# One kind of two-bank PSUM tile for an attention and gMLP stack, with the 64-row matmuls of the gMLP gathered into fewer runs

## The chip, the cores and the metric

The kernel runs on one core of one Trainium2 chip, in one launch. The metric is the device time in microseconds (us); the median of three runs of the kernel before is 1190.72 us (1190.54 to 1191.43). The engines are named as the profile names them: PE is TensorE (its matmuls), PEld its weight loads, DVE is VectorE, ACT is ScalarE, POOL is GpSimd, and SP issues DMAs.

## What is computed

Four layers on an activation x of 2048 rows by 576 columns, in the order A, B, A, B, with the same weights both times:

```python
x = x + _A_ref(_layernorm(x), A_wqkv, A_wo)
x = x + _B_ref(_layernorm(x), B_w_in, B_w_sp, B_b_sp, B_w_out)
x = x + _A_ref(_layernorm(x), A_wqkv, A_wo)
x = x + _B_ref(_layernorm(x), B_w_in, B_w_sp, B_b_sp, B_w_out)
```

Layer A is attention with 32 heads of 18 columns, in which each row looks at 8 earlier rows at a distance of 2. Layer B is a gMLP with Fh = 2304:

```python
z  = _gelu(x @ w_in)                 # 2048 x 4608
z1 = z[..., :Fh]
z2 = _layernorm(z[..., Fh:])
g  = einsum('ts,bsf->btf', w_sp, z2) + b_sp
return (z1 * g) @ w_out
```

## The kernel before

**Layer A** (`layer_A`) projects q and k (`PG`, tile `pp`) and v (`VW`, tile `pv`), and then walks through 38 half-steps, two for each of 19 row tiles. A half-step multiplies q and k into logits (`L_mm`, tiles `L_ps`), takes their exponential on ACT (`EXP`), multiplies by v (`PV`, tile `O_ps`), and fits in what is left of the projections and the output projection (`WO`, tile `pw`). The order of the instructions on each engine in layer A is the order in which the code is written (`tc.manual_schedule`).

**Layer B** (`layer_B`) has three stages. The first computes z2 for each of 16 tiles of 128 rows (`p1_main`, line 791), takes the gelu and sums on ACT (line 805), sums of squares on DVE (line 807) and ACT (line 809), and normalizes (`p1_norm`, DVE and POOL, lines 832 and 834). The second takes 9 blocks of 256 columns: z1 of a block with 128 columns at a time (`z1(jj, sub)`, line 869, gelu in line 881), and the spatial product for 512 rows at a time (`gate`, 16 matmuls in line 887, then two DVE instructions in lines 891 and 892). The third multiplies by w_out (`p3_mm`, line 941, tile `po`) and adds x (`p3_finish`, line 951). In layer B the framework's scheduler sets the order of the instructions.

**Semaphore waits** are drawn by the framework, which keeps account of which instruction reads and writes which tile. When a pool's slot is taken by a new tile, the first write to it waits until the last reader of the tile that was there before is through.

**PSUM** has 8 banks of 512 fp32 columns per partition. Here they are shared out once for the whole kernel: two slots of two banks (`H_tile`, tag "H", for `L_ps`, `pz`, `pz1`, `po2`), and four slots of one bank (`PT_tile`, tag "PT", for all else: `pp`, `pv`, `O_ps`, `pw`, the transposes `pt`, `pzs`, `pg`, `po`). Each `PT_tile` is a tile of its own. In layer A, 151 such one-bank tiles are written in the first layer and 146 in the second; most are read by a single DVE or ACT instruction, `O_ps` by two.

**The 64-row remainder.** The inner dimension of 576 is four times 128 and 64 more. The four full pieces are matmuls of 128 rows. [...] In the z2 stage a tile of 128 rows has five units (512, 512, 512, 512 and 256 columns): units 0 and 1 first with their full pieces, then the run of five remainders, then the full pieces of the other three. In z1 there are four units of 512 columns and a run of four remainders for each 128 columns.

Of the kernel before, what the change touches and what calls it, by code (L numbers as in the profile page):

```python
# [9 lines left out]
ACT = mybir.ActivationFunctionType  # L10
# [8 lines left out]
P = 128  # L19
D = 576  # L20
H = 32
# [41 lines left out]
class K:  # L63
# [135 lines left out]
    def H_tile(self, name):  # L199
        return self.ps.tile([P, 2, 512], f32, name=name, tag="H", bufs=2)  # L200

    def PT_tile(self, shape, dt, name):
        return self.ps.tile(shape, dt, name=name, tag="PT", bufs=4)
# [118 lines left out]
    def layer_A(self, li):  # L322
# [26 lines left out]
        if li == 0:  # L349
            w2 = R["win2a"][:].rearrange("p c n -> p (c n)")  # L350
            lent = [w2[:, k_ * 2 * CBW:(k_ + 1) * 2 * CBW].rearrange("p (a b) -> p a b", a=2) for k_ in range(2)]
        man = tc.manual_schedule(engines={ET.PE, ET.Activation, ET.DVE, ET.Pool, ET.SP})
# [370 lines left out]
    def layer_B(self, li):  # L723
# [7 lines left out]

        zu_cm = pool("zu")
# [19 lines left out]
        cchunks = []  # L752
        c0 = 0
        while c0 < Fh:
            cn = min(1024, Fh - c0)
            cchunks.append((c0, cn))
            c0 += cn
        ncch = len(cchunks)
        SQ_D = (Fh * 2 // 3) // 256 * 256
        units = []  # L760
        for ci, (c0, cn) in enumerate(cchunks):
            for sub in range((cn + 511) // 512):
                units.append((ci, c0, sub, min(512, cn - sub * 512)))
# [14 lines left out]
        def p1_main(i):  # L778
            zp = p1.tile([P, Fh], bf16, name="zp", bufs=3)
            sums = p1.tile([P, ncch + 2], f32, name="z_sums", bufs=3)  # L780
            pzvs = []
            for ci, (c0, cn) in enumerate(cchunks):
                if cn > 512:
                    pzvs.append(self.H_tile("pz")[:].rearrange("p a b -> p (a b)"))
                else:
                    pzvs.append(self.PT_tile([P, 512], f32, "pzs")[:, :])

            def z_mm(u, c, start, stop):
                ci, c0, sub, w = units[u]
                r0, r1 = (0, P) if c < 4 else (64 * (u % 2), 64 * (u % 2) + 64)  # L790
                nc.tensor.matmul(pzvs[ci][:, sub * 512:sub * 512 + w],  # L791
                                 lhsT=self.xnT[r0:r1, c, PADL + i * P:PADL + (i + 1) * P],
                                 rhs=win2(c)[r0:r1, c0 + sub * 512:c0 + sub * 512 + w],
                                 start=start, stop=stop, tile_position=(r0, 0))
            nu = len(units)
            for u in range(2):
                for c in range(4):
                    z_mm(u, c, c == 0, False)
            for u in range(nu):
                z_mm(u, 4, u >= 2, u < 2)  # L800
            for u in range(2, nu):
                for c in range(4):
                    z_mm(u, c, False, c == 3)
            for ci, (c0, cn) in enumerate(cchunks):
                nc.scalar.activation(out=zp[:, c0:c0 + cn], in_=pzvs[ci][:, 0:cn],  # L805
                                     func=ACT.Gelu_apprx_tanh, accum_out=sums[:, ci:ci + 1])
            nc.vector.tensor_tensor_reduce(out=spare[:, 0:SQ_D], in0=zp[:, 0:SQ_D], in1=zp[:, 0:SQ_D], scale=1.0,  # L807
                                           scalar=0.0, op0=ALU.mult, op1=ALU.add, accum_out=sums[:, ncch:ncch + 1])
            nc.scalar.activation(out=spare[:, SQ_D:Fh], in_=zp[:, SQ_D:Fh], func=ACT.Square,
                                 accum_out=sums[:, ncch + 1:ncch + 2])  # L810
            mean = p1.tile([P, 1], f32, name="z_mean", bufs=3)
            nc.vector.tensor_reduce(out=mean[:], in_=sums[:, 0:ncch], axis=AX.X, op=ALU.add)
# [5 lines left out]
            nc.vector.tensor_tensor(out=sq[:], in0=sums[:, ncch:ncch + 1], in1=sums[:, ncch + 1:ncch + 2], op=ALU.add)  # L818
# [18 lines left out]
        for i in range(NS):  # L837
            self.run_deferred(upto_row=(i + 1) * P)
            p1_main(i)
            if i == 0:  # L840
                self.run_deferred()
            if i == min(2, NS - 1):
                for q in range(NQ):
                    load_W(q)
                load_w1(0)
            if i == min(6, NS - 1):
                self.dma(bsp, self.B_b_sp.partition_broadcast(P), eng=nc.gpsimd)
            if i >= 1:
                p1_norm(i - 1)
# [11 lines left out]
        def z1(jj, sub):  # L861
            w1 = w1s[jj]
            z1T = p2.tile([P, S], bf16, name="z1T")
            z1Ts[jj, sub] = z1T
            pz1s = [self.H_tile("pz1") for _ in range(NQ // 2)]

            def mm(q, c, start, stop):
                r0, r1 = (0, P) if c < 4 else (64 * (q % 2), 64 * (q % 2) + 64)
                nc.tensor.matmul(pz1s[q // 2][:, q % 2, :], lhsT=w1[r0:r1, c, sub * P:(sub + 1) * P],  # L869
                                 rhs=self.xnT[r0:r1, c, PADL + q * 512:PADL + (q + 1) * 512],  # L870
                                 start=start, stop=stop, tile_position=(r0, 0))
            for q in range(2):
                for c in range(4):
                    mm(q, c, c == 0, False)
            for q in range(NQ):
                mm(q, 4, q >= 2, q < 2)
            for q in range(2, NQ):
                for c in range(4):
                    mm(q, c, False, c == 3)
            for q2 in range(0, NQ, 2):  # L880
                nc.scalar.activation(out=z1T[:, q2 * 512:(q2 + 2) * 512],  # L881
                                     in_=pz1s[q2 // 2][:, :, :].rearrange("p a b -> p (a b)"), func=ACT.Gelu_apprx_tanh)

        def gate(jj, sub, q):
            pg = self.PT_tile([P, 512], f32, "pg")
            for i in range(NS):
                nc.tensor.matmul(pg[:, :], lhsT=Z[:, jj, i, sub * P:(sub + 1) * P], rhs=Wq[q][:, i, :],  # L887
                                 start=(i == 0), stop=(i == NS - 1))
            qs = slice(q * 512, (q + 1) * 512)
            tmp = p2.tile([P, 512], f32, name="g_tmp", bufs=3)  # L890
            nc.vector.tensor_tensor(out=tmp[:], in0=pg[:, :], in1=bsp[:, qs], op=ALU.add)  # L891
            nc.vector.tensor_tensor(out=uT(jj)[:, sub, qs], in0=tmp[:], in1=z1Ts[jj, sub][:, qs], op=ALU.mult)  # L892

        for jj in range(NB):
            if jj + 1 < NB:
                load_w1(jj + 1)
            if 0 < jj < NB - 1:
                for sub in range(2):
                    z1(jj, sub)
                    for q in range(NQ):  # L900
                        gate(jj, sub, q)
            elif jj == 0:
                z1(jj, 0)
                z1(jj, 1)
                for sub in range(2):
                    for q in range(NQ):
                        gate(jj, sub, q)
            else:
                z1(jj, 0)
                z1(jj, 1)  # L910
                for q in range(NQ):
                    for sub in range(2):
                        gate(jj, sub, q)
# [48 lines left out]
        if NS >= 2 and JL > 0:  # L962
            accs = []
            for i in range(2):
                ht = self.H_tile("po2")
# [87 lines left out]
```

## The time and the profile before

| what | value |
|---|---|
| median of three runs | 1190.72 us |
| span of the profiled execution | 1190.8 us |
| mean granted TensorE clock | 0.998 |
| first layer A, 0 to about 136 us | PE busy 129.3 us |
| first layer B: z2 to 208.3, z1 and gates to 530.7, w_out to 601.4 us | PE busy throughout |
| second layer A, 601.4 to about 722 us | PE busy 119.7 of 120.6 us |
| second layer B: z2 to 794.7, z1 and gates to 1117.0, w_out to the end | PE busy throughout but for the last 3 us |

All the profile's figures are of one execution. A matmul's duration in it (379 ns for 512 columns) is longer than the distance from its start to the next one's, since matmuls overlap in the array; what a matmul costs is read from the distance between starts, or from a chain of many: 64 gate matmuls take 13.81 us there, 215.8 ns each. Idle time of an engine that nothing waits for costs nothing.

### The profile page before, as it was taken

What the parts mean: (1) busy time and instruction counts of PE and PEld (TensorE: products, weight loads), DVE (VectorE), ACT (ScalarE), POOL (GpSimd) and SP (SyncE); (2) the same over time, 40 slices, a digit from 0 to 9 for tenths busy, and PEclk for the clock granted to TensorE, in tenths of its full rate; (3) what the DMA queues carried; (4) which work ended last, traced back from release to release, by engine and by line L of the source; (5) the groups of instructions that cost most, each with busy time, mean ns of one, the idle gap of its engine ahead of it and who ended that gap; (6) DMA issues with size and microseconds to landing.
All of it is one profiled execution on the core that took longest, in us unless ns stands there. A gap on an engine that the chain in (4) does not pass through costs nothing.

```text
span 1190.8 us, 20761 instructions
## 1 busy us (share of the span) xinstructions
PE 1180.2 (99%) x8554; PEld 620.6 (52%) x8554; DVE 547.4 (46%) x1206; ACT 376.6 (32%) x593; POOL 281.5 (24%) x383
## 2 busy tenths in 40 slices
PE   8999999999999999999999999999999999999998
PEld 5567544444444444457755775444444444444677
DVE  8688587333233233245556786753233233233311
ACT  5578677210110110202156786760110110111000
POOL 4768685000000000001153877530000000000000
PEclk9999999999999999999999999999999999999999
DMA  8989992000000000049645999900000000000332
GB/s 195 200 163 199 181 224 65 23 4 9 12 12 12 12 1 11 12 139 291 169 98 117 203 227 196 202 14 9 12 12 1 12 12 12 12 1 28 125 105 73
DMA packets 178104, 101.21 MB, mean 85 GB/s; under 512 B 134336, under 2 KB 159360, under 8 KB 178009
## 3 DMA queue, kind: packets, MB, share of 16 engines
q1 hardware_dynamic: 165144, 78.13, 30.6%
q0 software_dynamic: 6512, 16.00, 5.4%
q10 hardware_dynamic: 6352, 5.75, 1.6%
q8 instruction: 67, 1.10, 0.4%
q14 instruction: 29, 0.23, 0.1%
HBM read 42.39 MB, written 16.53 MB: 49 GB/s over the span
## 4 chain that ended last, share of the span: by engine, by line
PE 94%; DMA 3%; POOL 1%; ACT 0%; issue 0%; SPq 0%; DVE 0%; ACTq 0%; DVEq 0%
PE pg L887 42%; PE pz L869 12%; PE po L941 12%; PE pz L791 11%; PE pp L402 5%; PE pw L494 3%; PE O_ps L457 3%; PE pv L379 3%; PE L_ps L437 2%; DMA oT<-o_t 2%; PE pzs L791 1%; DMA QK<-win2a 1%; POOL QK L77 1%; DMA wqk_sb<-in_A_wqkv_dram 1%; ACT P_sb L446 0%
## 5 line engine op out<-in xcount | busy, mean ns | idle before, releaser
L887 PE MATMUL pg<-Wq,Z 128*128 128x512 bf16 x2304 | 502.8, 379 | 0.0
L887 PEld LDWEIGHTS <-Z 128*128 128x128 bf16 x2304 | 225.3, 98 | 272.0
L891 DVE TENSOR_TENSOR g_tmp<-pg,ln_xn 128x512 f32<-128x512 f32 x144 | 99.6, 692 | 429.2 <-PE pg L887 429.2
L881 ACT ACTIVATE z1T<-pz 128x1024 bf16<-128x1024 f32 x72 | 73.7, 1024 | 513.8 <-PE pz L869 513.6
L77 POOL DMA_DIRECT2D wout<-in_B_w_out_dram x4 | 4.3, 1064 | 604.6 <-PE pg L887 604.6
L941 PE MATMUL po<-wout,Z 128*128 128x288 bf16 x1152 | 141.4, 286 | 0.0
L446 ACT ACTIVATE P_sb<-L_ps 128x896 bf16<-128x896 f32 (+1 forms) x152 | 126.7, 887 | 41.2 <-PE L_ps L437 40.6
L869 PE MATMUL pz<-xnT,w 128*128 128x512 bf16 (+1 forms) x640 | 136.0, 380 | 0.0
L941 PEld LDWEIGHTS <-Z 128*128 128x128 bf16 x1152 | 112.7, 98 | 28.8
L791 PEld LDWEIGHTS <-xnT 128*128 128x128 bf16 (+1 forms) x800 | 66.2, 97 | 81.0 <-issue 23.7
L791 PE MATMUL pz<-win2a,xnT 128*128 128x512 bf16 x384 | 104.8, 380 | 0.0
L892 DVE TENSOR_TENSOR Z<-g_tmp,z1T 128x512 bf16<-128x512 f32 x144 | 99.6, 692 | 9.7
L869 PEld LDWEIGHTS <-w 128*128 128x128 bf16 (+1 forms) x640 | 51.1, 97 | 80.0 <-issue 27.1
L402 PE MATMUL pp<-xnT,wqk_sb 128*128 128x512 bf16 x360 | 83.8, 382 | 0.5 <-DMA wqk_sb<-in_A_wqkv_dram 0.5
L805 ACT ACTIVATE zp<-pz 128x1024 bf16<-128x1024 f32 x64 | 65.5, 1024 | 36.6 <-PE pz L791 32.8
L951 DVE TENSOR_TENSOR x_new<-po,xo 128x288 f32<-128x288 f32 (+1 forms) x64 | 28.8, 455 | 87.6 <-PE po L941 83.5
L791 PE MATMUL pz<-win2b,xnT 128*128 128x512 bf16 (+1 forms) x256 | 65.7, 380 | 0.0
L807 DVE CUSTOM_DVE_ANT_0 Z<-zp 128x1536 bf16<-128x1536 bf16 x32 | 56.6, 1769 | 13.1 <-ACT zp L805 13.0
L77 POOL DMA_DIRECT2D QK<-stg x81 | 50.7, 631 | 36.3 <-DVE stg L371 21.0
L379 PE MATMUL pv<-wv_sb,xnT 128*128 128x288 bf16 (+1 forms) x380 | 55.8, 285 | 0.0
L242 POOL TENSOR_SCALAR ln_xn<-x_new,ln_mv,ln_rstd 128x576 bf16<-128x576 f32 x23 | 52.8, 2294 | 2.0
L402 PEld LDWEIGHTS <-wqk_sb 128*128 128x128 bf16 x360 | 33.2, 98 | 37.2 <-DMA wqk_sb<-in_A_wqkv_dram 1.0
(114 smaller groups left out, 916.9 us busy)
## 6 DMA issues: line engine op xcount, KB each, us to landing
xres<-x_new SPq DMA_DIRECT2D x48, 288.0 KB
xo<-xres SPq DMA_DIRECT2D x32, 288.0 KB
wout<-in_B_w_out_dram POOLq DMA_DIRECT2D x4, 1296.0 KB, 8.5
xo<-xres SPq DMA_DIRECT2D x8, 576.0 KB
w<-in_B_w_in_dram SPq DMA_DIRECT2D x16, 256.0 KB
QK<-stg POOLq DMA_DIRECT2D x53, 72.0 KB, 4.4
QK<-stg SPq DMA_DIRECT2D x41, 72.0 KB
xo<-in_A_x_dram SPq DMA_DIRECT2D x8, 288.0 KB
```

What stands on the lines that cost most here:

```text
L77: return eng.dma_start(out=out, in_=in_)
L379: nc.tensor.matmul(pv[:nk, 0:288], lhsT=self.xnT[:, c, QT * t:QT * t + nk], rhs=wv_sb[:, c, hh * 288:(hh + 1) * 288], start=(c == 0), stop ...
L402: nc.tensor.matmul(pp[:, :], lhsT=w, rhs=self.xnT[:, c, PADL + cc * 512:PADL + (cc + 1) * 512], start=(c == 0), stop=(c == 4))
L446: nc.scalar.activation(out=P_bufs[(2 * s + jp) % 4][:nk, :, :, 0:nq], in_=Lv[:nk, :, :, 0:nq], func=ACT.Exp, scale=scale)
L791: nc.tensor.matmul(pzvs[ci][:, sub * 512:sub * 512 + w], lhsT=self.xnT[r0:r1, c, PADL + i * P:PADL + (i + 1) * P], rhs=win2(c)[r0:r1, c0 + ...
L805: nc.scalar.activation(out=zp[:, c0:c0 + cn], in_=pzvs[ci][:, 0:cn], func=ACT.Gelu_apprx_tanh, accum_out=sums[:, ci:ci + 1])
L869: nc.tensor.matmul(pz1s[q // 2][:, q % 2, :], lhsT=w1[r0:r1, c, sub * P:(sub + 1) * P], rhs=self.xnT[r0:r1, c, PADL + q * 512:PADL + (q + ...
L881: nc.scalar.activation(out=z1T[:, q2 * 512:(q2 + 2) * 512], in_=pz1s[q2 // 2][:, :, :].rearrange("p a b -> p (a b)"), func=ACT.Gelu_apprx_ ...
L887: nc.tensor.matmul(pg[:, :], lhsT=Z[:, jj, i, sub * P:(sub + 1) * P], rhs=Wq[q][:, i, :], start=(i == 0), stop=(i == NS - 1))
L891: nc.vector.tensor_tensor(out=tmp[:], in0=pg[:, :], in1=bsp[:, qs], op=ALU.add)
L892: nc.vector.tensor_tensor(out=uT(jj)[:, sub, qs], in0=tmp[:], in1=z1Ts[jj, sub][:, qs], op=ALU.mult)
L941: nc.tensor.matmul(acc[hh], lhsT=uT(j // 2)[:, j % 2, i * P:(i + 1) * P], rhs=wouts[j // NJH][:, j % NJH, hh * 288:(hh + 1) * 288], start= ...
```

## The change

**PSUM is one tag of four slots of two banks** ("pair"). In layer A two of the four are taken at the start (`open_banks`) and held to the layer's end; `PT_tile` no longer makes a tile but returns one half of one of these two, in turn: tile 0's first bank, its second, tile 1's first, its second, and again. `L_ps` has the other two slots, as many as before.

**z2** is cut into units of two times 384 columns (three units for 128 rows, 48 in a layer). Four units form a group, which fills all eight banks: the full pieces of the first two units, then one run of eight remainders, then the full pieces of the other two. A gelu covers one unit of 768 columns. A row tile's sums and normalization follow its third unit; the loads of w_sp and b_sp are issued after the third and the sixth group.

**z1** does the whole block of 256 columns at once, four units of two times 512, with one run of eight remainders; the eight gates follow. Before, in all but the first and the last block, four gates stood between the two halves of z1.

**The gates** take one slot for two gates, one bank each. **The third stage** takes one slot for the two halves of a row tile, 288 columns in each bank.

```diff
     def H_tile(self, name):
-        return self.ps.tile([P, 2, 512], f32, name=name, tag="H", bufs=2)
+        return self.ps.tile([P, 2, 512], f32, name=name, tag="pair", bufs=4)
+
+    def open_banks(self):
+        self.banks = [self.H_tile("banks") for _ in range(2)]
+        self.bank_rr = 0
 
     def PT_tile(self, shape, dt, name):
-        return self.ps.tile(shape, dt, name=name, tag="PT", bufs=4)
+        k_ = self.bank_rr % 4
+        self.bank_rr += 1
+        t = self.banks[k_ // 2][:, k_ % 2, :]
+        if dt == f32:
+            return t
+        n = shape[1] * shape[2]
+        return t.bitcast(dt)[:, 0:n].rearrange("p (a b) -> p a b", a=shape[1])
...
+        self.open_banks()
         man = tc.manual_schedule(engines={ET.PE, ET.Activation, ET.DVE, ET.Pool, ET.SP})
...
+        PW = Fh // 6
+        NU = 3 * NS
...
+        def z_mm(u, pz, a_, c, start, stop):
+            i, p = divmod(u, 3)
+            r0, r1 = (0, P) if c < 4 else (64 * a_, 64 * a_ + 64)
+            c0 = (2 * p + a_) * PW
+            nc.tensor.matmul(pz[:, a_, 0:PW], lhsT=self.xnT[r0:r1, c, PADL + i * P:PADL + (i + 1) * P],
+                             rhs=win2(c)[r0:r1, c0:c0 + PW], start=start, stop=stop, tile_position=(r0, 0))
...
+        for k0 in range(0, NU, 4):
+            us = list(range(k0, min(k0 + 4, NU)))
+            self.run_deferred(upto_row=(us[-1] // 3 + 1) * P)
+            tl = {}
+            for u in us[:2]:
+                tl[u] = p1_open(u)
+                for a_ in range(2):
+                    for c in range(4):
+                        z_mm(u, tl[u], a_, c, c == 0, False)
+            for u in us:
+                if u not in tl:
+                    tl[u] = p1_open(u)
+                for a_ in range(2):
+                    z_mm(u, tl[u], a_, 4, u not in us[:2], u in us[:2])
+            for u in us[:2]:
+                p1_gelu(u, tl[u])
+            for u in us[2:]:
+                for a_ in range(2):
+                    for c in range(4):
+                        z_mm(u, tl[u], a_, c, False, c == 3)
+                p1_gelu(u, tl[u])
...
-        def z1(jj, sub):
+        def z1(jj):
             w1 = w1s[jj]
...
+            units = [(sub, q2, pair("pz1")) for sub in range(2) for q2 in range(0, NQ, 2)]
...
+            nu = len(units)
+            first = nu // 2
+            for u in range(first):
+                mains(u)
+            for u in range(nu):
+                for a_ in range(2):
+                    mm(u, a_, 4, u >= first, u < first)
+            for u in range(first):
+                gelu(u)
+            for u in range(first, nu):
+                mains(u)
+                gelu(u)
+
+        def gate(jj, sub, q, pg):
...
+            z1(jj)
+            order = ([(sub, q) for sub in range(2) for q in range(NQ)] if jj < NB - 1 else
+                     [(sub, q) for q in range(NQ) for sub in range(2)])
+            for k_, (sub, q) in enumerate(order):
+                if k_ % 2 == 0:
+                    pgs = pair("pg")
+                gate(jj, sub, q, pgs[:, k_ % 2, :])
...
         for i in range(i0, NS):
-            pos_ = [self.PT_tile([P, 512], f32, "po") for hh in range(2)]
-            acc = [pos_[0][:, 0:288], pos_[1][:, 0:288]]
+            pos_ = pair("po")
+            acc = [pos_[:, hh, 0:288] for hh in range(2)]
             p3_mm(i, acc, range(NJ))
             p3_finish(i, acc)
```

More of the change, by code (lines that the diff above doesn't have):

```diff
@@ L730, in pool @@
             return tc.tile_pool(name=f"B{li}_{name}", bufs=bufs, reuse_waits="tile")
+        pair = self.H_tile
         zu_cm = pool("zu")
@@ L751, in load_W @@
             nc.sync.dma_start_transpose(out=Wq[q][:], in_=self.B_w_sp[q * 512:(q + 1) * 512, :])
[L752 to L758, printed above, removed]
+        PW = Fh // 6
+        NU = 3 * NS
         SQ_D = (Fh * 2 // 3) // 256 * 256
[L760 to L763, printed above, removed]
         bsp = self.bsp
@@ L776, in layer_B @@
         zst = {}
[L778 to L806, printed above, removed]
@@ new lines, in layer_B, with p1_open @@
+        zps = {}
+        def p1_open(u):
+            i, p = divmod(u, 3)
+            if p == 0:
+                zps[i] = [p1.tile([P, Fh], bf16, name="zp", bufs=3), p1.tile([P, 8], f32, name="z_sums", bufs=3)]
+            return pair("pz")
+        def z_mm(u, pz, a_, c, start, stop):
+            i, p = divmod(u, 3)
+            r0, r1 = (0, P) if c < 4 else (64 * a_, 64 * a_ + 64)
+            c0 = (2 * p + a_) * PW
+            nc.tensor.matmul(pz[:, a_, 0:PW], lhsT=self.xnT[r0:r1, c, PADL + i * P:PADL + (i + 1) * P],
+                             rhs=win2(c)[r0:r1, c0:c0 + PW], start=start, stop=stop, tile_position=(r0, 0))
@@ L807, in p1_main, with p1_gelu, p1_stats @@
+        def p1_gelu(u, pz):
+            i, p = divmod(u, 3)
+            zp, sums = zps[i]
+            nc.scalar.activation(out=zp[:, 2 * p * PW:2 * (p + 1) * PW].rearrange("p (a b) -> p a b", a=2),
+                                 in_=pz[:, :, 0:PW], func=ACT.Gelu_apprx_tanh, accum_out=sums[:, p:p + 1])
+            if p == 2:
+                p1_stats(i)
+        def p1_stats(i):
+            zp, sums = zps.pop(i)
+            n = 3
             nc.vector.tensor_tensor_reduce(out=spare[:, 0:SQ_D], in0=zp[:, 0:SQ_D], in1=zp[:, 0:SQ_D], scale=1.0,
-                                           scalar=0.0, op0=ALU.mult, op1=ALU.add, accum_out=sums[:, ncch:ncch + 1])
+                                           scalar=0.0, op0=ALU.mult, op1=ALU.add, accum_out=sums[:, n:n + 1])
@@ L809, in p1_main @@
             nc.scalar.activation(out=spare[:, SQ_D:Fh], in_=zp[:, SQ_D:Fh], func=ACT.Square,
-                                 accum_out=sums[:, ncch + 1:ncch + 2])
+                                 accum_out=sums[:, n + 1:n + 2])
             mean = p1.tile([P, 1], f32, name="z_mean", bufs=3)
-            nc.vector.tensor_reduce(out=mean[:], in_=sums[:, 0:ncch], axis=AX.X, op=ALU.add)
+            nc.vector.tensor_reduce(out=mean[:], in_=sums[:, 0:n], axis=AX.X, op=ALU.add)
             nc.vector.tensor_scalar_mul(out=mean[:], in0=mean[:], scalar1=1.0 / Fh)
@@ L817, in p1_main @@
             sq = p1.tile([P, 1], f32, name="z_sq", bufs=3)
-            nc.vector.tensor_tensor(out=sq[:], in0=sums[:, ncch:ncch + 1], in1=sums[:, ncch + 1:ncch + 2], op=ALU.add)
+            nc.vector.tensor_tensor(out=sq[:], in0=sums[:, n:n + 1], in1=sums[:, n + 1:n + 2], op=ALU.add)
             rstd = p1.tile([P, 1], f32, name="z_rstd", bufs=3)
@@ L835, in p1_norm @@
                                     scalar2=nmr[:, 0:1], op0=ALU.mult, op1=ALU.add)
[L837 to L840, printed above, removed]
+        for k0 in range(0, NU, 4):
[19 more added lines that the diff above has]
+                p1_gelu(u, tl[u])
+            if k0 == 0:
                 self.run_deferred()
-            if i == min(2, NS - 1):
+            if k0 == 8:
                 for q in range(NQ):
@@ L845, in layer_B @@
                 load_w1(0)
-            if i == min(6, NS - 1):
+            if k0 == 20:
                 self.dma(bsp, self.B_b_sp.partition_broadcast(P), eng=nc.gpsimd)
-            if i >= 1:
-                p1_norm(i - 1)
+            for i in sorted(zst):
+                if 3 * (i + 1) + 2 <= us[-1]:
+                    p1_norm(i)
         p1_norm(NS - 1)
@@ L859, in layer_B, with mm @@
         z1Ts = {}
-        def z1(jj, sub):
+        def z1(jj):
             w1 = w1s[jj]
[L863 to L869, printed above, removed]
+            for sub in range(2):
+                z1Ts[jj, sub] = p2.tile([P, S], bf16, name="z1T")
+            units = [(sub, q2, pair("pz1")) for sub in range(2) for q2 in range(0, NQ, 2)]
+            def mm(u, a_, c, start, stop):
+                sub, q2, pz1 = units[u]
+                q = q2 + a_
+                r0, r1 = (0, P) if c < 4 else (64 * a_, 64 * a_ + 64)
+                nc.tensor.matmul(pz1[:, a_, :], lhsT=w1[r0:r1, c, sub * P:(sub + 1) * P],
@@ L870, in mm @@
                                  rhs=self.xnT[r0:r1, c, PADL + q * 512:PADL + (q + 1) * 512],
                                  start=start, stop=stop, tile_position=(r0, 0))
[L872 to L882, printed above, removed]
@@ L884, in gate, with mains, gelu @@
-        def gate(jj, sub, q):
-            pg = self.PT_tile([P, 512], f32, "pg")
+            def mains(u):
+                for a_ in range(2):
+                    for c in range(4):
+                        mm(u, a_, c, u < first and c == 0, u >= first and c == 3)
+            def gelu(u):
+                sub, q2, pz1 = units[u]
+                nc.scalar.activation(out=z1Ts[jj, sub][:, q2 * 512:(q2 + 2) * 512],
+                                     in_=pz1[:, :, :].rearrange("p a b -> p (a b)"), func=ACT.Gelu_apprx_tanh)
@@ L886, in gate @@
+            nu = len(units)
[3 more added lines that the diff above has]
+            for u in range(nu):
+                for a_ in range(2):
+                    mm(u, a_, 4, u >= first, u < first)
[5 more added lines that the diff above has]
+        def gate(jj, sub, q, pg):
             for i in range(NS):
-                nc.tensor.matmul(pg[:, :], lhsT=Z[:, jj, i, sub * P:(sub + 1) * P], rhs=Wq[q][:, i, :],
+                nc.tensor.matmul(pg, lhsT=Z[:, jj, i, sub * P:(sub + 1) * P], rhs=Wq[q][:, i, :],
@@ L890, in gate @@
             tmp = p2.tile([P, 512], f32, name="g_tmp", bufs=3)
-            nc.vector.tensor_tensor(out=tmp[:], in0=pg[:, :], in1=bsp[:, qs], op=ALU.add)
+            nc.vector.tensor_tensor(out=tmp[:], in0=pg, in1=bsp[:, qs], op=ALU.add)
             nc.vector.tensor_tensor(out=uT(jj)[:, sub, qs], in0=tmp[:], in1=z1Ts[jj, sub][:, qs], op=ALU.mult)
@@ L896, in layer_B @@
                 load_w1(jj + 1)
[L897 to L913, printed above, removed]
+            z1(jj)
[5 more added lines that the diff above has]
+                gate(jj, sub, q, pgs[:, k_ % 2, :])
         p2_cm.__exit__(None, None, None)
@@ L964, in layer_B @@
             for i in range(2):
-                ht = self.H_tile("po2")
+                ht = pair("po2")
                 accs.append([ht[:, 0, 0:288], ht[:, 1, 0:288]])
```

## The prediction

> **What bounds the kernel now.** First the page's engine totals and its chain of waits:
>
> ```profile
> PE 1180.2 (99%) x8554; PEld 620.6 (52%) x8554; DVE 547.4 (46%) x1206; ACT 376.6 (32%) x593; POOL 281.5 (24%) x383
> ...
> PE 94%; DMA 3%; POOL 1%; ACT 0%; issue 0%; SPq 0%; DVE 0%; ACTq 0%; DVEq 0%
> ```
>
> PE is the bound in every stage, so an edit is worth what it takes from PE's order, and costs every wait that it puts into it. How little PE waits now stands in the view of waits for PE, whose largest rows are:
>
> ```profile
> PE pw L494 <- DMA oT<-o_t: 1.8, 2, 1.2
> PE L_ps L437 <- ACT P_sb L446: 1.6, 5, 0.4
> PE warm L541 <- POOL ident L184: 1.5, 1, 1.5
> ```
>
> The six rows of that view sum to 7.3 us. Next, the chain in order of time, in the gates (start, length, what):
>
> ```profile
> 244.29 4.10 PE pz L869 x20
> 248.39 13.81 PE pg L887 x64
> 262.20 4.10 PE pz L869 x20
> ```
>
> A gate matmul of 512 columns costs 13.81/64 = 0.2158 us. A z1 half (16 full matmuls, 4 remainders that go as 2 pairs) should cost 18 x 0.2158 = 3.884 and costs 4.10: **a run of 64-row matmuls costs about 0.21 us extra**. Single starts show where: 0.096 entering, 0.010 at the first pair, 0.092 leaving, 0.010 at the next full one. The timeline of the z2 stage has the same run, with its weight loads not hidden:
>
> ```profile
> 173.01 0.33 PEld L791 LDWEIGHTS <-xnT 64*128 64x128 bf16 x5 [0.42 <-issue]
> ...
> 173.65 3.57 PEld L791 LDWEIGHTS <-xnT 128*128 128x128 bf16 x20 [0.32 <-issue]
> ...
> 177.65 0.33 PEld L791 LDWEIGHTS <-xnT 64*128 64x128 bf16 x5 [0.42 <-issue]
> ```
>
> A row tile of z2 takes 177.65 - 173.01 = 4.64 us.
>
> **z1, and what it saves.** 18 runs in a layer become 9; a run of four pairs costs its overhead once. 18 runs fewer in two layers x 0.21 = **-3.8 us**.
>
> **z2, and what it saves.** 384 columns lie between 256 (starts 0.1094 apart) and 512 (0.2159): 0.1626. A group is 32 full matmuls (5.20), four pairs (4 x 0.165 = 0.66) and one overhead (0.21): 6.07 us for four units, 4.55 for a row tile. 32 row tiles x 0.09 = **-2.9 us**. The weight load (98 ns) stays under 163, as it does under the 123 of the third stage's matmuls. Around it: a gelu of 768 columns lies between 0.38 (256) and 1.02 (1024), about 0.81, so ACT has some 3.75 us of work in 4.55 (3 x 0.81, 3 x 0.1 to read the sums out, 1.03 for the square), and DVE's and POOL's chain from one sum of squares to the next takes 4.10 (157.21 to 161.31) in 4.55. PE has four slots where it had two and a bit, and the first unit's slot is free over a microsecond before the next group asks. I take no wait here. If POOL's late first normalization (DVE idles 6.0 us for it at 148) bites, gelu's `zp` buffers are what is late next: gelu already idles 1.02 us at 151 and PE has 1.9 us of slack there; that could give back 0 to 2 us.
>
> **Gates and third stage.** Same matmuls. The loads of w_sp, later by at most one row tile (4.6 us), are needed after 208 and the DMA engines are quiet from about 180. In the third stage two halves become one tile and the first half's addition moves behind the second half's matmuls; only at the kernel's end does that show, one DVE addition, **+0.4** (0.456).
>
> **The waits that the change adds.** Whether a slice of a two-bank tile is as good as a tile of its own depends on how the program's waits are drawn. The kernel before has one place where the two banks of a tile are read separately: the first two row tiles of the third stage (`po2`).
>
> ```profile
> 530.69 14.50 PE L941 MATMUL po<-wout,Z 128*128 128x288 bf16 x117
> ...
> 539.22 0.82 DVE L951 TENSOR_TENSOR x_new<-po,xo 128x288 f32<-128x288 f32 x2 [5.58 <-PE po L941]
> ```
>
> Starts are 0.1225 apart and a matmul takes 0.286. The first bank is complete after 66 matmuls: 530.69 + 65 x 0.1225 + 0.286 = 538.94. The second, after 68: 539.19. DVE had idled 5.58 us and begins with the *first* bank at 539.22, after the *second* is done; PE's semaphore is raised at the 68th matmul and not at the 66th, and the same in the last layer (1125.58). The order at 530.69 says it again: after nine matmuls PE should go on with bank 2 of row tile 0 while half of w_out is missing, but the tenth (531.79) waits for ACT anew, as only the other slot has to: it is row tile 1. So in this program **the two banks of a PSUM tile count as one** for the waits: a write to one waits for the readers of the other. (SBUF tiles do go by region: DVE's line 807 starts at 199.94 on `zp` while gelu still writes its last columns, 199.81 to 200.19.)
>
> In layer A this means that each second-bank tile waits until the first-bank tile just before it is evacuated. From the timeline:
>
> ```profile
> 61.94 0.56 PE L457 MATMUL O_ps<-v_ext,P_sb 128*128 128x19 bf16 x16
> 62.36 1.24 PE L402 MATMUL pp<-xnT,wqk_sb 128*128 128x512 bf16 x5
> ...
> 62.83 0.46 DVE L464 TENSOR_TENSOR o_t<-O_ps,rec 112x288 bf16<-112x288 f32 x1
> 63.53 0.67 PE L437 MATMUL L_ps<-QK 32*128 32x112 bf16 x16
> 63.70 0.69 DVE L371 CAST stg<-pp 128x512 bf16<-128x512 f32 x1 [0.41 <-PE pp L402]
> 64.14 0.56 PE L457 MATMUL O_ps<-v_ext,P_sb 128*128 128x19 bf16 x16
> ```
>
> If `O_ps` is first and `pp` second, `pp` at 62.36 waits until 63.29 and a signal of 0.04: 0.97 us. If `pp` is first, `O_ps` at 64.14 waits until 64.40: 0.30. The order is written out, so nothing is put in between: behind the waiting matmul stand all of PE's later ones, with EXP and the evacuations behind those. I numbered the one-bank tiles in PE's order, as the slots go round, and took for each even one the time from the next one's first matmul to the end of its reader plus 0.04. The low end leaves out queueing on DVE and ACT (last matmul's end, 0.04, the reader's own time, 0.04); the high end takes the reader's end as traced:
>
> - 40 `pv` first: 23.5 low, 30.7 high
> - 34 `pp`: 25.4, 28.8
> - 39 `O_ps`: 37.2, 47.9
> - 30 `pw`: 8.0, 10.9 (`L_mm` covers most)
> - 4 transposes: 2.6, 2.6
>
> Together 96.6 to 120.9 us. First-bank tiles wait for the reader three tiles back, 2.9 us in all by the trace and less once PE is slower: 0. With PE waiting, the queues on DVE and ACT shrink, so I take a third of the difference; of the 7.3 us that PE waits already I let 4 be swallowed: 96.6 + 8 - 4 = **+100 us**.
>
> The gates have the same wait: the second gate of a pair behind DVE's line 891 on the first, 0.379 - 0.216 + 0.04 + 0.692 + 0.04 = 0.93 us, 72 times, 67 us if bare. But layer B's order comes from a scheduler, and it fills:
>
> ```profile
> 212.41 0.81 PE L887 MATMUL pg<-Wq,Z 128*128 128x512 bf16 x3
> ...
> 213.05 4.26 PE L869 MATMUL pz<-xnT,Z 128*128 128x512 bf16 x20
> ```
>
> Three gate matmuls were put ahead of z1's second half. Four to five matmuls of the next pair cover 0.93 (4 x 0.216 leaves 0.07): 0 to 5 us, taken as **+2.5**. Without that cover it is the 67.
>
> Sum: 1190.8 - 3.8 - 2.9 + 0.4 + 100 + 2.5 = **1287**. Span and median differ by 0.1 us, so this stands for the median too.
>
> [...] The rows at 539.22 and 1125.58 show a wait in the program where the banks differ, so I go by them.
>
> The granted clock was halved once, for 3.41 us from 50.5, after two microseconds in which PE streamed columns 39% of the time; with 100 us of waits layer A would still stream about 70%, so I count nothing, and leave up to 5 us in the range. [...]
>
> **The rivals.** *Waits go by bank*, and the order at 531.79 has another cause: then only the savings are left, 1184, faster. For it: SBUF tiles go by region. Against: both `po2` places. It decides at the first `pp` after an `O_ps` in layer A. *The gates aren't filled*: 1287 + 64 = 1351; for it, a scheduler's order is right only if its own idea of DVE's time is; against it, the three hoisted matmuls. *Layer A has more slack than the waits show*, half of the added time being swallowed: about 1237; against it, 99% PE. *The smaller units don't save* (384 columns not side by side): 1294, inside the range.
>
> **How the numbers follow.** The forecast, waits by tile with gates filled, 0.81; by bank 0.10; gates bare 0.06; swallowed 0.03. The range of the forecast: low, all of the 7.3 us swallowed, no queueing, no gate loss, and 10 for waits that overlap each other in ways that the sum can't see: 1190.8 - 6.3 + 96.6 - 7.3 - 10 = 1264; high, 120.9, 5 at the gates, 5 for the clock: 1190.8 - 6.3 + 130.9 = 1315. That holds 0.8 alone, and the other cases are left out. Less than 0.2% (2.4 us) can't be told from no change: faster 0.10, same 0.01, slower 0.89.
>
> **What would show it.** PE's idle time in layer A rises to about 100 us, with `O_ps`, `pp` and `pv` readers (lines 371, 373, 464) as releasers, and the layers take 180 and 175 us in place of 136 and 121; a z2 group takes 6.07 us and z1 7.99 a block (8.20 before); gates of a pair are interleaved with the next pair's. I am wrong if PE starts the second bank's matmuls while DVE reads the first.

## The result, and the profile after

| | median, us | runs | ratio to before |
|---|---|---|---|
| before | 1190.72 | 5 | 1 |
| after | 1303.86 (1303.56 to 1306.72) | 5 | 1.0943 [1.0922, 1.0965] |

The kernel became 9.4% slower; 1287 was forecast, with 1264 to 1315 as the range. The profiled execution after the change has a span of 1303.6 us, against 1190.8. By stage, between first matmuls; only into and out of a layer A the border is the start of the last matmul before it and of its own last one, since a few matmuls of z2 already run among its last ones:

| us | layer A | z2 | z1, gates | w_out | layer A | z2 | z1, gates | w_out, end |
|---|---|---|---|---|---|---|---|---|
| before | 135.0 | 73.3 | 322.4 | 70.4 | 120.3 | 73.3 | 322.4 | 73.8 |
| after | 177.7 | 70.8 | 324.3 | 70.4 | 191.3 | 70.6 | 324.3 | 74.3 |
| difference | +42.7 | -2.5 | +1.9 | 0 | +71.0 | -2.7 | +1.9 | +0.5 |

The whole loss is in the two layers A: +113.7 of +112.8 us. From the page after, its engine totals, two rows of its slices, and its chain:

```profile
PE 1199.5 (92%) x8714; PEld 640.7 (49%) x8714; DVE 544.8 (42%) x1206; ACT 372.3 (29%) x593; POOL 296.1 (23%) x383
...
PE   7777699999999999999977666999999999999998
...
PEclk9998999999999999999999988899999999999999
...
PE 84%; DVE 7%; issue 3%; ACT 2%; POOL 2%; DMA 1%; DVEq 0%; SPq 0%; POOLq 0%; ACTq 0%
```

PE fell from 99% to 92% of a longer span, and DVE, which had 0% of the chain, has 7%: the chain now goes through the readers of PSUM. The slices put the gaps into the two stretches of layer A, and in the same places PEclk drops below 9. The view of waits for PE names the readers (us in total, times, longest):

```profile
PE banks L390 <- DVE o_t L475: 26.8, 23, 1.6
PE banks L413 <- DVE o_t L475: 13.3, 14, 1.6
PE banks L413 <- ACT stg L384: 9.8, 14, 1.0
PE banks L505 <- DVE v_ext L382: 9.0, 13, 1.1
PE banks L505 <- ACT v_ext L384: 6.1, 11, 0.8
PE banks L468 <- DVE x_new L508: 5.8, 21, 1.2
```

`pv` (L390), `pp` (L413), `pw` (L505) and `O_ps` (L468) wait for `o_t`, `stg`, `v_ext` and `x_new`, which read the *other* bank. The view of before had no wait for the reader of another bank among its rows, which sum to 7.3 us; those of after sum to about 100. The plainest place is the start of the second layer A, where only `pp` tiles of five matmuls run. The chain in order of time:

```profile
649.64 2.33 PE banks L413 x10
...
651.99 0.59 ACT stg L384
...
652.63 2.33 PE banks L413 x10
...
654.98 0.59 ACT stg L384
...
655.62 2.33 PE banks L413 x10
```

Ten matmuls are two tiles of work: the second bank of one PSUM tile, whose first bank has just been read, and the first bank of the next. The matmul after those wants the second bank of that tile, and PE stands 0.66 us (651.97 to 652.63) until ACT has read the first. The bank that it wants was free all that time: DVE's read of its last contents ended at 648.25. In a full half-step of layer A, PE's own timeline (start, length, instruction; in brackets the idle time before it and what ended it) reads:

```profile
705.34 1.24 PE L413 MATMUL banks<-xnT,wqk_sb 128*128 128x512 bf16 x5 [0.84 <-DVE o_t L475]
706.52 0.40 PE L448 MATMUL L_ps<-QK 32*128 32x112 bf16 x16
706.85 0.56 PE L468 MATMUL banks<-v_ext,P_sb 128*128 128x19 bf16 x16
708.25 0.77 PE L390 MATMUL banks<-wv_sb,xnT 128*128 128x288 bf16 x5 [0.84 <-DVE o_t L475]
708.95 0.40 PE L448 MATMUL L_ps<-QK 32*128 32x112 bf16 x16
709.28 0.57 PE L468 MATMUL banks<-v_ext,P_sb 128*128 128x19 bf16 x16
710.69 1.74 PE L413 MATMUL banks<-xnT,wqk_sb 128*128 128x512 bf16 x4 [0.84 <-DVE o_t L475]
```

Each `O_ps` (L468) is followed by 0.84 us of nothing, while DVE divides it. The last row shows a second thing: four matmuls in 1.74 us instead of about 1.03 (280.96, further down). Here the granted clock is halved (0.51 from 710.8 to 714.3). What the two effects come to, in layer A's windows of before (the first two rows) and after:

```profile
0.00:135.00 135.00, 128.26 (x1826) 82.90 (x1827) 107.00 (x304) 90.42 (x125) 90.65 (x144) 0.99 0.96 189
601.40:721.65 120.25, 119.38 (x1763) 76.63 (x1761) 84.41 (x221) 86.26 (x125) 77.55 (x97) 1.00 0.81 168
```

```profile
0.00:177.70 177.70, 134.44 (x1834) 84.19 (x1835) 109.17 (x304) 91.03 (x125) 86.83 (x143) 0.98 0.65 148
643.40:834.70 191.30, 136.31 (x1782) 81.00 (x1781) 86.99 (x223) 87.94 (x125) 78.16 (x98) 0.93 0.48 108
...
772.30:789.40 17.10, 13.27 (x168) 7.93 (x165) 6.15 (x17) 7.76 (x11) 5.95 (x7) 0.50 0.55 130
```

The columns are the window, its length, busy time of PE, PEld, DVE, ACT and POOL, the granted clock, the DMA share and GB/s. PE's idle time in layer A goes from 6.7 + 0.9 to 43.3 + 55.0 us, that is +90.6. Its busy time rises by 6.2 + 16.9 = 23.1. The halved clock held for 34.1 us (3.4 at 116.9, 123.8 and 710.9, 17.1 at 772.3, 6.8 at 816.7), with PE busy for 28.0 of them; at twice the speed that is at most 14 us less. About another 2.4 is work of z2 that is now mixed into layer A's end (z2's stages lost 5.2 where the instructions explain 2.8; 13 and 24 of z2's matmuls start before layer A's last one, and 5 and 5 before the change). The last 6.7 would fit matmuls whose full length shows where a wait follows them (379 ns against 216 between starts); that was not separated further.

### The profile page after: what moved, and what is told of

It is laid out like the page before. It is cut to its first block, busy times and chain, and to the rows that moved or that the text cites. A ratio compares the mean times of both kernels' runs of the same rounds, so it can differ in the third digit from the quotient of the medians.

```text
span 1303.6 us, 21091 instructions
## 1 busy us (share of the span) xinstructions
PE 1199.5 (92%) x8714; PEld 640.7 (49%) x8714; DVE 544.8 (42%) x1206; ACT 372.3 (29%) x593; POOL 296.1 (23%) x383
## 4 chain that ended last, share of the span: by engine, by line
PE 84%; DVE 7%; issue 3%; ACT 2%; POOL 2%; DMA 1%; DVEq 0%; SPq 0%; POOLq 0%; ACTq 0%
PE pg L918 39%; PE pz L890 11%; PE po L962 11%; PE pz L793 10%; PE banks L413 6%; PE banks L390 3%; PE banks L505 3%; PE banks L468 2%; DVE o_t L475 2%; POOL ln_xn L252 2%; DVE ln_st L227 1%; DVE x_new L508 1%; DVE rec L474 1%; DVE stg L382 1%; PE L_ps L448 1%
## 5 line engine op out<-in xcount | busy, mean ns | idle before, releaser
L890 PE MATMUL pz<-xnT,w 128*128 128x512 bf16 (+1 forms) x640 | 132.9, 379 | 0.0
L962 PEld LDWEIGHTS <-Z 128*128 128x128 bf16 x1152 | 112.7, 98 | 28.8
L793 PE MATMUL pz<-win2a,xnT 128*128 128x384 bf16 x576 | 126.3, 326 | 0.4 <-ACT zp L799 0.4
L413 PE MATMUL banks<-xnT,wqk_sb 128*128 128x512 bf16 x360 | 86.6, 381 | 30.7 <-DVE o_t L475 13.3
L793 PEld LDWEIGHTS <-xnT 128*128 128x128 bf16 (+1 forms) x960 | 80.4, 97 | 65.4 <-issue 16.8
L390 PE MATMUL banks<-wv_sb,xnT 128*128 128x288 bf16 (+1 forms) x380 | 61.7, 301 | 34.2 <-DVE o_t L475 26.8
L799 ACT ACTIVATE zp<-pz 128x768 bf16<-128x768 f32 x96 | 76.7, 804 | 36.8 <-PE pz L793 26.0
L793 PE MATMUL pz<-win2b,xnT 128*128 128x384 bf16 (+1 forms) x384 | 81.3, 326 | 0.4 <-ACT zp L799 0.4
L505 PE MATMUL banks<-wo_sb,oT 128*128 128x288 bf16 x320 | 53.1, 301 | 19.0 <-DVE v_ext L382 9.0
L413 PEld LDWEIGHTS <-wqk_sb 128*128 128x128 bf16 x360 | 34.2, 97 | 71.8 <-issue 38.7
L232 POOL TENSOR_TENSOR ln_rstd<-ln_rstd,neg_half 128x1 f32<-128x1 f32 x48 | 26.8, 558 | 172.1 <-DVE ln_rstd L231 146.9
```

Source lines behind the costliest of these rows:

```text
L390: nc.tensor.matmul(pv[:nk, 0:288], lhsT=self.xnT[:, c, QT * t:QT * t + nk], rhs=wv_sb[:, c, hh * 288:(hh + 1) * 288], start=(c == 0), stop ...
L413: nc.tensor.matmul(pp[:, :], lhsT=w, rhs=self.xnT[:, c, PADL + cc * 512:PADL + (cc + 1) * 512], start=(c == 0), stop=(c == 4))
L505: nc.tensor.matmul(pw[:, 0:288], lhsT=oT[:, c, r0:r0 + P], rhs=wo_sb[:, c, hh * 288:(hh + 1) * 288], start=(c == 0), stop=(c == 4))
L793: nc.tensor.matmul(pz[:, a_, 0:PW], lhsT=self.xnT[r0:r1, c, PADL + i * P:PADL + (i + 1) * P], rhs=win2(c)[r0:r1, c0:c0 + PW], start=start, ...
L799: nc.scalar.activation(out=zp[:, 2 * p * PW:2 * (p + 1) * PW].rearrange("p (a b) -> p a b", a=2), in_=pz[:, :, 0:PW], func=ACT.Gelu_apprx_ ...
L890: nc.tensor.matmul(pz1[:, a_, :], lhsT=w1[r0:r1, c, sub * P:(sub + 1) * P], rhs=self.xnT[r0:r1, c, PADL + q * 512:PADL + (q + 1) * 512], s ...
```

## The experiments

Each ratio is to the kernel before, run beside it.

**Another turn through the banks.** One line of the kernel after: neighbours in PE's order come from different PSUM tiles, and each tile waits for the reader two back instead of the one just before.

```diff
-        t = self.banks[k_ // 2][:, k_ % 2, :]
+        t = self.banks[k_ % 2][:, k_ // 2, :]
```

> The changed kernel, but layer A's one-bank tiles go round as tile 0 first bank, tile 1 first bank, tile 0 second bank, tile 1 second bank. Nothing else differs: the same two held tiles, the same four banks, the same order on PE. Theory (the program's waits count both banks of a tile as one): each one-bank tile now waits for the reader two tiles back and not for the one just before it. From the trace of the kernel before, the time from a tile's first matmul to the end of the reader two tiles back sums to 19 us without queueing and 52 us with the queueing as traced, over both layers, against 97 and 121 for the neighbour; so about 1191 + 1 + 19 to 52 = 1210 to 1243 us, nearer the low end, about 1218. Rival (what costs is that the four banks are held or that the slots go round in a fixed order, or something in layer B): no change, 1304 us.

1222.72 us, 1.0253 [1.0238, 1.0267]; layers A take 145.1 and 140.3, everything else stays. The waits that are left:

```profile
PE banks L505 <- DVE o_t L475: 20.0, 35, 1.0
PE L_ps L448 <- ACT P_sb L457: 2.2, 6, 0.4
PE banks L390 <- DVE x_new L508: 2.1, 3, 0.8
```

The same banks, matmuls and readers, in the same order, but 81 us less. The large row is now the tile two after `O_ps`, and of the 40.1 us of `pp` and `pv` behind `o_t` 0.9 is left. In the windows of both layers A the granted clock is 1.00, so some of the 81 us is the clock's. If waits went by bank, the turn could not matter.

**Own tiles in layer A.** The kernel after, with a PSUM pool for each layer: layer A has its four one-bank tiles back, layer B keeps the four pairs. These pools have the option `reuse_waits="tile"`, which the pool before lacks; the last experiment has the pools and nothing else.

```diff
-        return self.ps.tile([P, 2, 512], f32, name=name, tag="pair", bufs=4)
+        return self.ps.tile([P, 2, 512], f32, name=name, tag="pair", bufs=2 if self.in_A else 4)
...
     def PT_tile(self, shape, dt, name):
-        k_ = self.bank_rr % 4
...
+        return self.ps.tile(shape, dt, name=name, tag="PT", bufs=4)
...
+        with tc.tile_pool(name=f"ps{li}", bufs=1, space=PSUM, reuse_waits="tile") as k.ps:
```

> The changed kernel, but PSUM is shared out anew for each layer: layer A has two two-bank slots and four one-bank tiles of their own, as before the change, layer B has the changed kernel's four two-bank slots. Layer B's code is the changed one. Theory: all of layer A's 113 us go away, and what is left is layer B's: z2 -2.9 us over both layers, z1 -3.8, the gates 72 x 0.083 = +6.0 (the start gap of 298 ns in place of 216 at each second gate of a pair), the end +0.5; together 1190.7 - 0.2 = 1190.5 us, between 1189 and 1192. Rival (part of the loss is layer B's new order or its eight full banks): 1200 us or more.

1196.18 us, 1.0034 [1.0021, 1.0047]; layers A take 133.4 and 120.7 again, so all of their loss was in the tiles. But the time is 4 us above the kernel before, where a small gain was expected: the stage of z1 and gates keeps its +1.9 in each layer, and z2 shows no gain (73.1 and 73.2). The last experiment here bears on the latter.

**Own slots for the gates.** The kernel of the experiment just before, with a two-bank slot for each gate, one bank of it unused.

```diff
-                if k_ % 2 == 0:
-                    pgs = pair("pg")
-                gate(jj, sub, q, pgs[:, k_ % 2, :])
+                gate(jj, sub, q, pair("pg")[:, 0, :])
```

> As the run with PSUM shared out for each layer, and in addition each gate has a two-bank slot to itself and uses its first bank. Theory: the start gap of 298 ns at each second gate goes away, 72 x 0.083 = 6.0 us less than with PSUM shared out alone: 1184.5 us. Rival (the gap is that of PE's switching from one weight source or bank to another, and stays): the same time as that run.

1187.65 us, 0.997 [0.9952, 0.9987]; z1 and gates take 320.49 in each layer, 3.77 less than with paired gates and 1.89 less than before. Against the experiment just before the time is 8.5 us less, where 6.0 was expected; the stages explain 7.5 of it. Its chain in a block has no interleaving left, and eight gates take 27.63 us, 215.9 ns a matmul:

```profile
246.07 7.98 PE pz L878 x40
254.05 27.63 PE pg L906 x128
281.68 7.98 PE pz L878 x40
```

**Halves in layer A, and nothing else.** The kernel before, with a PSUM pool for each layer; in layer A the one-bank tiles are halves of two held tiles, taken in turn as the change does. Layer B is that of before.

```diff
-        return self.ps.tile([P, 2, 512], f32, name=name, tag="H", bufs=2)
+        return self.ps.tile([P, 2, 512], f32, name=name, tag="H", bufs=4 if self.in_A else 2)
...
+        if not self.in_A:
+            return self.ps.tile(shape, dt, name=name, tag="PT", bufs=4)
+        k_ = self.bank_rr % 4
+        self.bank_rr += 1
+        t = self.banks[k_ // 2][:, k_ % 2, :]
```

> The kernel before, with one edit: in layer A the one-bank tiles are halves of two held two-bank tiles, in the changed kernel's order. Layer B is that of before. PSUM is shared out anew for each layer. Theory: this alone makes the loss, 1190.7 + 113 = 1304 us, with PE waiting in layer A for DVE and ACT readers of the neighbour bank. Rival (the loss needs layer B's part too): clearly less, 1250 us or below.

1319.36 us, 1.1054 [1.1024, 1.1084]. One edit makes the whole loss, and more: the waits are those of after to within a few tenths in their main rows (27.0, 13.3, 9.8 in the three largest), but layers A take 178.3 and 197.7, the second 6.4 more than in after. The granted clock of that execution is 0.976, which over its span of 1317.8 us is some 63 us at half speed; by the same sum the 0.987 of after is some 34.

**Only z1.** The kernel before, with z1 of a block in one run; its first two units go to `H` tiles, the other two to four `PT` tiles, and the gates keep a tile each.

```diff
+    def unit(self, k, name):
+        if k < 2:
+            t = self.H_tile(name)
+            return [t[:, 0, :], t[:, 1, :]], t
+        return [self.PT_tile([P, 512], f32, name)[:, :] for _ in range(2)], None
...
-            for q in range(2):
-                for c in range(4):
-                    mm(q, c, c == 0, False)
...
+            for u in range(first):
+                mains(u)
+            for u in range(nu):
+                for a_ in range(2):
+                    mm(u, a_, 4, u >= first, u < first)
```

> The kernel before, with its own one-bank tiles everywhere, and one edit: z1 of a 256-column block is done at once with one run of eight remainders, its first two units in the two two-bank slots and the other two in four one-bank tiles (with a gelu of 512 columns each); the eight gates follow, each in its own one-bank tile. Theory: 18 runs of 64-row matmuls fewer at 0.21 us, -3.8 us, with nothing given back at the gates: 0.9968 of the time before, and 320.5 us for z1 and gates in each layer in place of 322.4. Rival (the new order of z1 and gates costs something of its own): no gain.

1189.13 us, 0.9967 [0.9954, 0.9981]; 320.49 in each layer against 322.38. So z1 alone is worth 2 x 1.89 = 3.8 us.

**z1 and z2, with tiles of their own.** The same, and z2 in units of two times 384 columns, four to a run, again two in `H` tiles and two in `PT` tiles. Layer A, the gates and the third stage are those of before.

```diff
+            return self.unit(u % 4, "pz")
...
+            nc.tensor.matmul(pz[0][a_][:, 0:PW], lhsT=self.xnT[r0:r1, c, PADL + i * P:PADL + (i + 1) * P],
+                             rhs=win2(c)[r0:r1, c0:c0 + PW], start=start, stop=stop, tile_position=(r0, 0))
```

> As the run with the new z1, and z2 too in the changed kernel's units of 2 x 384 columns and groups of four, the first two units of a group in the two-bank slots and the other two in four one-bank tiles (a gelu of 384 columns each, so ACT has about 0.4 us more in a row tile's 4.55). Every tile that is read by itself is a tile of its own. Theory: -3.8 - 2.9 = -6.7 us, 0.9944 of the time before, and the saving of the z2 stage survives because layer A's end and the first units of z2 still mix on PE. Rival (z2's saving is lost at the border, or ACT becomes the bound): 0.9968 or above.

1185.37 us, 0.9931 [0.9909, 0.9953]: the best version, with both savings and none of the waits. In the profile z2 takes 71.91 in each layer (73.28 before), z1 and gates 320.49, and the span is 1184.2, 6.6 less than before.

**Filler in the waits.** The kernel after, with two matmuls of 208 columns, whose result nobody reads, put into `O_ps`'s bank in nearly every half-step: 140 in all, which at 0.2158 us for 512 columns are 12.3 us of PE. If the halved clock comes from thin streaming, filler should keep it full.

```diff
             O_ps = self.PT_tile([P, 512], f32, "O_ps")
+            if s >= 3:
+                for _ in range(2):
+                    nc.tensor.matmul(O_ps[:, 304:512], lhsT=wo_sb[:, 0, 0:P], rhs=wo_sb[:, 0, 0:208], start=True, stop=True)
```

> The changed kernel with two matmuls more in each of layer A's half-steps from the fourth on: 208 columns each into the unused end of O_ps's bank, read by nobody. Their PE time is 35 x 2 x 2 x 0.089 = 12.5 us. Theory (the clock was halved in layer A because PE streamed less than some 40% of a 3.4 us window, and not because it stood still for long): the halved windows (34 us in the changed kernel's profile, worth up to about 14 us) mostly vanish and the time stays within some 5 us of the changed kernel's 1304, though PE does 12.5 us more. Rival (the halved clock has nothing to do with how much PE streams): as many halved windows and 1316 us or more.

1317.88 us, 1.1033 [1.0989, 1.1076]: a median between two groups, and so no answer. Two executions took 1322 us at a granted clock of 0.980, which is 53 us of half speed; the other two took 1309.63 and 1313.72 at 0.992 and 0.990, which is 21 and 26 us, less than the 29 to 34 us of the kernel after (0.989 to 0.987). The first two fit the other side's forecast, and the 1309.63 nearly the theory's. The profiled execution is one of the first two: in it the waits hardly shrank (25.0, 12.9 and 9.8 in the largest rows, against 26.8, 13.3 and 9.8 in after), and the filler lengthened the steps. So this doesn't tell what rules the clock.

**Only the pools.** The kernel before with nothing but a PSUM pool for each layer, as the second and the fourth experiment use it.

```diff
-        self.ps = ctx.enter_context(tc.tile_pool(name="ps", bufs=1, space=PSUM))
...
+        with tc.tile_pool(name=f"ps{li}", bufs=1, space=PSUM, reuse_waits="tile") as k.ps:
```

> The kernel before, with PSUM shared out anew for each layer and nothing else changed (same slots, same tiles). Theory (the runs with PSUM shared out for each layer came out some 3 to 5 us above the sum because z2's first matmuls can no longer be mixed into layer A's end): 2 to 5 us slower than before, with the loss between layer A's last half-steps and the end of z2. Rival (a border between PSUM pools costs nothing): the same time as before.

1194.31 us, 1.0011 [0.9994, 1.0027]: no difference that this can tell. But its stages move: layers A 131.1 and 119.7, z2 74.4 and 74.7. So the border that a pool draws takes work of z2 out of layer A's end: no matmul of z2 starts before layer A's last one, where 5 did. Against these z2's, the second experiment's 73.1 and 73.2 are 1.2 and 1.5 less, which fits a saving in z2 that the border hid. It isn't shown: layer A and z2 together take 206.5 and 193.9 us there and 205.4 and 194.4 here, so their sum has no such saving, and the 2 us between the two medians stay unexplained.

## Why the prediction was right

**Waits in layer A: +100 forecast, +91 to +97 found.** The idle time rose by 90.6 us; with the 6.7 beside it, if they belong to it, this is 97.3. The readers are those that were named. By reader, the rows of the view of waits sum to 40.1 us behind `O_ps` (37.2 to 47.9 forecast), 23.4 behind `pp` (25.4 to 28.8), 21.5 behind `pv` (23.5 to 30.7), 7.1 behind `pw` (8.0 to 10.9) and 2.0 behind the transposes (2.6): the low ends were nearly right, and most of the queueing above them did not come. That two banks of a tile count as one was read from two places in the third stage; another turn through the same banks took 81 us away, and halves in layer A alone brought the whole loss back. The wait is the program's, not the banks': in the best version, as in before, `pp`, `O_ps`, `pv` and `pw` go through four tiles of one bank each, and PE fills one while DVE and ACT read its neighbours: in before PE writes `pp` from 62.36 to 63.60 while DVE reads `O_ps` from 62.83 to 63.29, and `pp` from 12.68 to 13.92 while ACT reads `pv` from 12.88 to 13.28.

**The sum without the waits**, 1184, the figure of the rival by which waits go by bank, is close to the best version's 1185.37. There the banks are tiles of their own, and in the change they weren't.

**z1: -3.8, exact.** It is hidden in after by the gates, and bare in the experiment on z1 alone: 3.78.

**z2: -2.9 forecast, -2.7 found** (two times 1.37 in the best version). A group took the 6.07 us worked out for it: the run of eight remainders with one full matmul behind it, in PE's timeline after, comes every 6.06. In the run the two 64-row matmuls of a pair start 0.003 to 0.004 us apart (196.635 and 196.639 in the first pair), and the next pair 0.16 to 0.17 later. So the 384 columns do go side by side, and that rival falls; its 1294 doesn't follow from the prediction's own numbers either (four pairs more of 0.163 in each of 24 groups are some 16 us, which makes 1303).

```profile
196.38 1.08 PE L793 MATMUL pz<-win2b,xnT 128*128 128x384 bf16 x9
...
202.44 1.08 PE L793 MATMUL pz<-win2b,xnT 128*128 128x384 bf16 x9
...
208.50 1.08 PE L793 MATMUL pz<-win2b,xnT 128*128 128x384 bf16 x9
```

**The end: +0.4 forecast, +0.5 found.** DVE's two additions stand together at 1300.08, behind the last matmul, and take 0.82 us.

**Gates: right mechanism, wrong size, +2.5 forecast and +7.5 found.** The scheduler filled each wait with four matmuls of the next work, as said. In the timeline after, first an inner pair and then a layer's last:

```profile
280.96 1.03 PE L890 MATMUL pz<-xnT,w 128*128 128x512 bf16 x4
281.16 0.69 DVE L922 TENSOR_TENSOR g_tmp<-pg,ln_xn 128x512 f32<-128x512 f32 x1 [1.17 <-PE pg L918]
...
281.91 3.61 PE L918 MATMUL pg<-Wq,Z 128*128 128x512 bf16 x16
...
569.32 3.61 PE L918 MATMUL pg<-Wq,Z 128*128 128x512 bf16 x16 [0.78 <-DVE g_tmp L922]
```

From 280.96 to 281.91 four matmuls take 0.95 us and cost 0.86: 0.09 is left, and it is the wait: DVE's read of the first gate ends at 281.85, and the second gate starts 0.06 later. The prediction had this (0.07), but it took half of it as a mean, where every pair pays it. 72 x 0.083 (the start gap of 298 ns instead of 216) = 6.0. The last pair of each layer has nothing behind it to fill with and pays 0.78. Together 7.5, and giving each gate its own slot took back 2 x 3.77 = 7.5. The upper bound of 5 was too low, and this eats more than z1's whole saving.

**The clock: nothing forecast, about 13 us found.** This is the step that failed. Executions of one kernel price it: with halves in layer A alone the granted clock went from 0.982 to 0.972 and the span from 1311.4 to 1321.1 us, and with filler from 0.992 to 0.980 and from 1307.9 to 1320.4. As an estimate from these, that is some 0.4 us for each us at half speed, and 13 for the 34 of after. The step rested on the author's estimate that layer A would still stream columns 70% of the time, and that was too high: worked out from the starts and columns of its matmuls (as in the last section here), PE streamed 59% of the first layer A (from 20 us on) and 56% of the second; before it was 78% and 82%. The prediction's own lengths, 180 and 175 us in place of 136 and 121, thin those to 59% and 57%. Nor do the 39% that it read before the one halving stand at its end: the last two microseconds before 50.5 have 51%, and the last 3.41 have 44%. Nor was the longest wait a sign of it: none in after was longer than 1.7 us, and the clock halved five times. With 13 in the place of 0, and 7.5 in the place of 2.5, the sum would have been 1305, against 1303.6.

**Why the range held.** The mechanism was right, but the range held in part by luck. Gates and clock went some 10 us over the 5 and 5 that it left for them; the room came from the queueing in its upper bound (120.9 where 91 to 97 were found), which was there for another reason.

## What to carry to other kernels

Before two PSUM tiles are merged into one, ask at which grain the program's waits are drawn: where they go by tile, a tile's second bank waits for the first one's reader, and what counts is which tile stands next in the engine's written order. Where halves must be shared, neighbours in that order should come from different tiles: one line, worth 81 of 113 us here. And when many waits of a microsecond are added to an engine that was dense, price the clock too: here it cost about 13 us, with no wait over 1.7 us, and in after each halving followed 3.41 us in which PE streamed 30 to 40% of the time, so the sparsest few microseconds told more than the longest gap.

## What the runs showed of the hardware

In after the granted clock was 0.50 in five stretches: 3.41 us from 116.93, from 123.76 and from 710.85, 17.07 us from 772.29 and 6.83 us from 816.66, which are one, one, one, five and two times 3.41. In before it was one stretch of 3.41 us, from 50.52, apart from the last 0.3 us of the execution. Cut into pieces of 3.41 us that start with those stretches, the two executions show the share of time in which PE streamed columns (a matmul's columns at 2.37 a nanosecond from its start, as 512 in 215.8 ns, and at half that where the clock is halved, where the matmuls from 711.37 to 712.22 start 0.43 us apart; overlaps counted once). It sorts the pieces of after, but not those of both together. In after the five pieces just ahead of a halved clock had shares of 0.30 to 0.40, and the sparsest that kept the clock had 0.42. In before the one halving followed a piece of 0.44, and the next sparsest, at 0.45, kept the clock. The profiled executions of the other turn through the banks and of the pools alone had a granted clock of 1.00 throughout. Full speed came back after halved pieces of 0.76 to 0.87, and the clock stayed halved after pieces of 0.38 to 0.69.

That looks like a wide band in which either state lasts, but at half speed the same columns fill twice the time. Counted at 2.37 a nanosecond in both states, the halved pieces after which full speed came back have 0.38 to 0.48, and those after which it stayed halved 0.24 to 0.37. Either way, what followed one sparse piece at 768.9 in after was 17.1 us of half speed. These are shares read from two traces; no run here set them by hand, and the one that tried to lift them did not settle it.
